# Late x and u tiles transposed by DMA from SBUF to SBUF, and constant matmuls in long planned TensorE gaps

## The chip, the cores and the metric

One core of one Trainium2 chip. The metric is the device time of one execution in microseconds (us). Executions of the same kernel differ by 2 to 3% here: the kernel before gave 174.18 to 178.64 us in its first four runs. Each run lists its granted TensorE clock and is called fast or slow (over 1.5% above the fastest of its kernel is slow).

## The reference, cut to what matters

A linear attention (4 batches, 8 heads, 768 steps, head size 48), whose output `x` goes through a mixing layer:

```python
y[:, :, t] = einsum(rt, state + (u * kt) vt);  state = wt * state + kt vt     # attention, S = 768
theta = x @ w_theta                                                          # needs x transposed
zr, zi = x * cos(theta), x * sin(theta)
u = x + w_tok_r @ zr + w_tok_i @ zi                                          # over the 768 steps
return u + maximum(u @ w_ch, 0)                                              # needs u transposed
```

The kernel works on 24 chunks of 128 steps (batch b, chunk c; number 6b + c). Each gives one x tile of 128x384 and later one u tile of 128x384. Both must be transposed, as three blocks of 128x128, before the product with `w_theta` or `w_ch`.

Of the kernel before, what the change touches and what calls it, by code (L numbers as in the profile page):

```python
# [43 lines left out]
class Planner:  # L44
# [10 lines left out]
    @staticmethod  # L55
    def key(name):

        kind = re.match("[a-zA-Z]+", name).group(0)
        num = name[len(kind):]
        if kind in ("tok", "un", "ut", "uc", "ml", "fin", "st"):  # L60
            b = int(num[0])
        else:
            b = int(num) // 6 if num and kind not in ("wt", "cwt", "wtr", "wev") else 1
        return kind + "@" + "0113"[min(b, 3)]
# [120 lines left out]
def kernel(  # L185
# [60 lines left out]
    sbp = ctx.enter_context(tc.tile_pool(name="sbp", bufs=1))
# [32 lines left out]
    P = Planner(SLOTS, SHIFT, PENALTY, SLACK)  # L279
# [50 lines left out]
    st = [dict() for _ in range(NT)]  # L330
# [24 lines left out]
    def mk_pair(m_, name, src):  # L355
        b, c = chunks[2 * m_]
# [3 lines left out]
        bf = [Buf(pool, [L, H, D], f32, refs=4 if name in "rk" else 2) for _ in range(2)]  # L360
# [6 lines left out]
        def fn():  # L367
# [32 lines left out]
    def attention(n):  # L400
# [189 lines left out]
        def f_xt():  # L590
            t = get(tx)
            for j in range(NJ):
                nc.tensor.transpose(t[:, j, :], x_all[:, b, c, j * L:(j + 1) * L], ident)  # L593
        o_xt = P.op("PE", 0.17, f_xt, [o_x], [tx, xT], [], prio=pr + OFF["xt"], name=f"xt{n}")

        def f_xc():
            nc.scalar.activation(get(xT), get(tx), AF.Copy)  # L597

        def f_xc_v():
            nc.vector.tensor_copy(get(xT), get(tx))  # L600
        s["o_xc"] = P.op("ACT", 0.38, f_xc, [o_xt], [], [tx], prio=pr + OFF["xc"], name=f"xc{n}",
                         alts=[("DVE", 0.26, f_xc_v, PEN)])
        s["o_x"] = o_x


    def attention_pair(m_):
# [181 lines left out]
        for g, hs in enumerate(halves):  # L788
# [10 lines left out]
            if not last:  # L799
# [99 lines left out]
    def mixing(b, ti):  # L899
# [26 lines left out]
        def f_ut():  # L926
            for j in range(NJ):
                nc.tensor.transpose(get(tx)[:, j, :], get(un)[:, j * L:(j + 1) * L], ident)  # L928
        o_ut = P.op("PE", 0.17, f_ut, [o_un], [tx, uT], [], prio=-1.0, name=f"ut{b}{ti}")

        def f_uc():
            nc.scalar.activation(get(uT), get(tx), AF.Copy)  # L932
# [108 lines left out]
```

## The kernel before: the parts that the change touches

Every piece of work is an operation of a planner: engine, planned duration, dependencies, buffers. The planner simulates the engines with these durations and emits the instructions in that order. In the traces here each engine then runs its own list in that order: TensorE stands still in front of a product that isn't ready (up to 2.5 us in the changed kernel) and doesn't pass it.

```python
LAG = {"PE": 0.21, "ACT": 0.16, "DVE": 0.14, "POOL": 0.10, "SP": 1.5, ...}   # after an operation's end
# ---- an x tile: three transposes on TensorE into PSUM, then a copy to SBUF
def f_xt():
    for j in range(NJ):                                   # NJ = 3
        nc.tensor.transpose(t[:, j, :], x_all[:, b, c, j * L:(j + 1) * L], ident)
o_xt = P.op("PE", 0.17, f_xt, [o_x], [tx, xT], [], ...)
s["o_xc"] = P.op("ACT", 0.38, f_xc, [o_xt], [], [tx], ..., alts=[("DVE", 0.26, f_xc_v, PEN)])
...                                                       # a u tile: the same, from un to uT
# ---- constant matmuls, in issue(): only `lead` = 33 at the start, as FUNTIL = 0
if o.start < until:
    n = min(int(gap * part / 0.056), -(-(target - seen) // 128))
    ...                                                   # (cut) a special rule for the first FCOLD us
    for _ in range(n):
        fill()                                            # 128x128 of zeros, result never read
```

All loads (but two of 1.5 KB), and the stores of the output, are issued by SP's queue: the loads for the attention, the weights, and one store for each u tile.

## Time and profile before

| | kernel before |
|---|---|
| median of the runs on record | 176.13 us (174.18 to 178.64, 4 runs; 174.72 over the first three, which the prediction knew) |
| span in the trace | 175.3 us, mean clock 0.941 (a slow run, 177.04 us) |
| TensorE busy | 158.7 us (91%) |
| last issue of a load | 120.2 us |

The busy rows, windows and groups are shown inside the prediction. Two more parts of the page matter for what follows: the chain of work that ended last, by engine, and the DMA issues (issuer, kind, count, size of each, median us from issue to landing).

```profile
PE 63%; DVE 12%; ACT 12%; DMA 8%; issue 1%; SPq 0%; ACTq 0%; DVEq 0%
...
out_dram<-sb_o SPq DMA_DIRECT2D x24, 192.0 KB, 2.0
in_w<-in_w_dram SPq DMA_DIRECT2D x18, 192.0 KB, 5.3
in_r<-in_r_dram SPq DMA_DIRECT2D x18, 192.0 KB, 4.5
```

`SPq` is the queue that issues DMAs.

### The profile page before, as it was taken

What the parts mean: (1) busy time and instruction counts of PE and PEld (TensorE: products, weight loads), DVE (VectorE), ACT (ScalarE), POOL (GpSimd) and SP (SyncE); (2) the same over time, 40 slices, a digit from 0 to 9 for tenths busy, and PEclk for the clock granted to TensorE, in tenths of its full rate; (3) what the DMA queues carried; (4) which work ended last, traced back from release to release, by engine and by line L of the source; (5) the groups of instructions that cost most, each with busy time, mean ns of one, the idle gap of its engine ahead of it and who ended that gap; (6) DMA issues with size and microseconds to landing.
All of it is one profiled execution on the core that took longest, in us unless ns stands there. A gap on an engine that the chain in (4) does not pass through costs nothing.

```text
span 175.3 us, 4898 instructions
## 1 busy us (share of the span) xinstructions
PE 158.7 (91%) x1919; PEld 104.7 (60%) x1919; DVE 130.5 (74%) x278; ACT 117.7 (67%) x255; POOL 114.0 (65%) x134
## 2 busy tenths in 40 slices
PE   7699898999759999999977999999899999999980
PEld 7257565776536566776643667666566666566640
DVE  4507869797996899867899399869989884645461
ACT  2469689799996987966988049799986924810000
POOL 7388689989759578559799987999789310000000
PEclk9858699999996999999996599999999999999999
DMA  5999998899999999999999979989011012112212
GB/s 115 272 301 264 215 222 203 218 264 238 262 222 256 284 160 309 211 208 197 214 206 192 189 129 199 204 174 217 12 45 46 9 38 76 62 45 90 95 45 90
DMA packets 93768, 29.81 MB, mean 170 GB/s; under 512 B 88369, under 2 KB 92210, under 8 KB 93746
## 3 DMA queue, kind: packets, MB, share of 16 engines
q1 hardware_dynamic: 93344, 29.50, 75.9%
q8 instruction: 15, 0.25, 0.6%
q10 hardware_dynamic: 402, 0.00, 0.1%
q14 instruction: 7, 0.06, 0.1%
HBM read 24.78 MB, written 4.72 MB: 168 GB/s over the span
## 4 chain that ended last, share of the span: by engine, by line
PE 63%; DVE 12%; ACT 12%; DMA 8%; issue 1%; SPq 0%; ACTq 0%; DVEq 0%
PE bank L914 24%; DVE sb_z L891 7%; PE bank L941 6%; DMA sb_w<-in_moe_w_tok_i_dram 4%; PE cum L646 3%; PE bank L877 3%; DMA in_k<-in_k_dram 2%; DMA in_w<-in_w_dram 2%; PE bank L928 2%; PE bank L509 2%; PE bank L572 2%; ACT sb_a L439 2%; PE bank L491 2%; PE bank L493 2%; PE cum L430 2%; PE bank L593 1%
## 5 line engine op out<-in xcount | busy, mean ns | idle before, releaser
L914 PE MATMUL bank<-sb_z,wtokT 128*128 128x384 bf16 x288 | 56.3, 337 | 0.4 <-DVE sb_z L891 0.4
L914 PEld LDWEIGHTS <-wtokT 128*128 128x128 bf16 x288 | 27.2, 100 | 17.5 <-issue 3.2
L485 POOL TENSOR_TENSOR sb_bon<-sb_v,sb_rub 128x384 bf16<-128x384 bf16 x18 | 14.9, 829 | 15.0 <-ACT sb_v L465 8.4
L891 DVE TENSOR_TENSOR sb_z<-x_all,sb_sc 128x768 bf16<-128x768 bf16 x24 | 21.6, 911 | 2.4 <-ACT sb_sc L885 2.4
L923 DVE TENSOR_TENSOR sb_un<-bank,x_all 128x384 bf16<-128x384 f32 x24 | 13.3, 555 | 12.2 <-PE bank L914 12.1
L452 POOL TENSOR_TENSOR sb_k<-in_k,sb_a 128x384 bf16<-128x384 f32 x18 | 19.2, 1069 | 4.7 <-DMA in_k<-in_k_dram 4.7
L476 POOL TENSOR_TENSOR sb_ruk<-sb_ru,in_k 128x384 bf16<-128x384 f32 x18 | 19.2, 1067 | 0.6
L458 POOL TENSOR_TENSOR sb_q<-in_r,sb_a 128x384 bf16<-128x384 f32 x18 | 19.0, 1055 | 0.9 <-DMA in_r<-in_r_dram 0.9
L469 POOL TENSOR_TENSOR sb_ru<-in_r,u_bc 128x384 f32<-128x384 f32 x18 | 18.9, 1051 | 0.0
L439 ACT ACTIVATE sb_a<-cum 128x768 f32<-128x768 f32 x18 | 14.6, 810 | 6.0 <-PE cum L434 5.7
L326 ACT ACT_TABLE_LOAD x12 | 15.4, 1283 | 1.5 <-PEq L1025 1.3
L941 PE MATMUL bank<-wch,sb_uT 128*128 128x384 bf16 x72 | 15.7, 326 | 0.6 <-DVE sb_uT L935 0.6
L946 DVE SCALAR_TENSOR_TENSOR sb_o<-bank,sb_un 128x384 f32<-128x384 f32 x24 | 13.3, 553 | 3.9 <-PE bank L941 3.9
L882 ACT ACTIVATE sb_sc<-bank 128x384 bf16<-128x384 f32 x24 | 12.2, 510 | 4.1 <-PE bank L877 4.1
L932 ACT ACTIVATE sb_uT<-bank 128x384 bf16<-128x384 bf16 x16 | 7.8, 489 | 10.3 <-PE bank L928 10.1
L885 ACT ACTIVATE sb_sc<-bank,hpi 128x384 bf16<-128x384 f32 x24 | 14.6, 607 | 0.0
L877 PE MATMUL bank<-wth,sb_xT 128*128 128x384 bf16 x72 | 14.0, 326 | 0.4 <-DVE x_all L841 0.4
L497 DVE COPY sb_qkt<-bank 128x1024 bf16<-128x1024 bf16 x18 | 12.3, 683 | 1.3 <-PE bank L493 1.1
L514 DVE TENSOR_TENSOR sb_p<-bank,mask_exc 128x512 bf16<-128x512 f32 x18 | 12.3, 681 | 0.9 <-PE bank L509 0.8
L521 DVE TENSOR_TENSOR sb_p<-bank,mask_exc 128x512 bf16<-128x512 f32 x18 | 12.2, 679 | 0.0
L587 DVE TENSOR_TENSOR x_all<-bank,sb_bon 128x192 bf16<-128x192 f32 x36 | 10.9, 346 | 1.3 <-PE bank L572 1.3
L597 ACT ACTIVATE sb_xT<-bank 128x384 bf16<-128x384 bf16 x18 | 8.8, 495 | 4.3 <-PE bank L593 4.2
(131 smaller groups left out, 337.1 us busy)
## 6 DMA issues: line engine op xcount, KB each, us to landing
out_dram<-sb_o SPq DMA_DIRECT2D x24, 192.0 KB, 2.0
in_w<-in_w_dram SPq DMA_DIRECT2D x18, 192.0 KB, 5.3
in_r<-in_r_dram SPq DMA_DIRECT2D x18, 192.0 KB, 4.5
in_k<-in_k_dram SPq DMA_DIRECT2D x18, 192.0 KB, 4.5
in_v<-in_v_dram SPq DMA_DIRECT2D x18, 192.0 KB, 4.6
sb_w<-in_moe_w_tok_r_dram SPq DMA_DIRECT2D x6, 384.0 KB, 4.7
sb_w<-in_moe_w_tok_i_dram SPq DMA_DIRECT2D x6, 384.0 KB, 5.1
in_w<-in_w_dram SPq DMA_DIRECT2D x3, 384.0 KB, 5.1
```

The costliest lines, as they stand in the source:

```text
L326: nc.scalar.preload_act_table_set(name)
L439: nc.scalar.activation(get(a), get(cum)[:, :, :DM], AF.Exp)
L452: nc.gpsimd.tensor_tensor(get(kk)[:, :, :D], s["x_k"](), av(1), op=ALU.mult)
L458: nc.gpsimd.tensor_tensor(get(q)[:, :, :D], s["x_r"](), av(0), op=ALU.mult)
L469: nc.gpsimd.tensor_tensor(get(ru), s["x_r"](), u_bc, op=ALU.mult)
L476: nc.gpsimd.tensor_tensor(get(ruk), get(ru), s["x_k"](), op=ALU.mult)
L485: nc.gpsimd.tensor_tensor(get(bon), get(vb), get(rub).to_broadcast([L, H, D]), op=ALU.mult)
L877: nc.tensor.matmul(get(th), lhsT=get(s["xT"])[:, j, :], rhs=wth[:, j, :], start=(j == 0), stop=(j == NJ - 1))
L885: nc.scalar.activation(get(sc)[:, 0, :], get(th), AF.Sin, bias=hpi)
L891: nc.vector.tensor_tensor(get(zb[b])[:, c], xb, get(sc), op=ALU.mult)
L914: nc.tensor.matmul(get(ac), lhsT=wtokT[:, q_, s_, ti, :], rhs=get(zb[b])[:, s_, q_, :], start=(s_ == 0 and q_ == 0), stop=(s_ == NCH - 1 a ...
L941: nc.tensor.matmul(get(ml), lhsT=get(uT)[:, j, :], rhs=wch[:, j, :], start=(j == 0), stop=(j == NJ - 1))
```

## The change

Its intent: take 17 of 48 tiles' transposes off TensorE, the busiest engine, and use the DMA path, which is nearly idle late in the kernel; and keep TensorE's clock up through long gaps. The tuned priorities were searched anew around it.

```diff
-    FCOLD, FPART, FSPAN, FCOL, FUNTIL = 16.0, 0.6, 1.7, 2250, 0.0
+    FCOLD, FPART, FSPAN, FCOL, FUNTIL = 0.0, 0.5, 3.4, 4600, 130.0     # constant matmuls in gaps
+    XBAR = (11, 22)        # u tiles by DMA
+    XBARX = (16, 22)       # x tiles by DMA
+        def f_xx():
+            for j in range(NJ):
+                nc.sync.dma_start(out=get(xT)[:, j, :], in_=x_all[:, b, c, j * L:(j + 1) * L], transpose=True)
+        if XBARX[0] <= n < XBARX[1]:
+            s["o_xc"] = P.op("SP", 0.9, f_xx, [o_x], [xT], [], ...)
+        else: ...          # as before
+        def f_ux():        # the same for u
+        if XBAR[0] <= b * NCH + ti < XBAR[1]:
+            o_uc = P.op("SP", 0.9, f_ux, [o_un], [uT], [], ...)
-    SHIFT, PENALTY, SLACK, WIN = ...          # (cut) the tuned constants of the planner,
+    SHIFT, PENALTY, SLACK, WIN = ...          # new values
-    sb_xT 9, sb_un 3, sb_uT 3                 # buffers
+    sb_xT 7, sb_un 4, sb_uT 4
```

Two planned durations were corrected too (a pair load 1.46 to 1.6 us, a state update 0.45 to 0.76 us).

More of the change, by code (lines that the diff above doesn't have):

```diff
@@ L59, in key @@
         num = name[len(kind):]
-        if kind in ("tok", "un", "ut", "uc", "ml", "fin", "st"):
+        if kind in ("tok", "un", "ut", "ux", "uc", "ml", "fin", "st"):
             b = int(num[0])
@@ L212 @@
     OFF = {'ln': -2.2, 'cum': -2.1, 'exp': -2.05, 'alt': -2.04, 'q': -1.5, 'k': -1.45, 'v': -1.2, 'ru': -1.3, 'ruk': -1.2, 'rub': -1.2, 'bon': -1.1, 'tqk': -0.9, 'qkt': -0.9, 'p': -0.8, 'm0': -0.7, 'pc': -0.7, 'sel': -1.6, 'y': -0.5, 'x': -0.5, 'xt': -0.4, 'xc': -0.4, 'rk': -1.3, 'rkt': -1.2, 'rkc': -1.2, 'beta': -1.15}
-    SHIFT = {'M': -0.23, 'M@0': 3.78, 'M@1': -3.52, 'M@3': 2.56, 'Mp@0': 0.29, 'S': -3.32, 'S@0': 0.3, 'S@1': -2.09, 'S@3': -3.9, 'Sp@0': -0.07, 'alt': -2.71, 'alt@0': -4.19, 'alt@1': -3.75, 'alt@3': -2.44, 'bc@0': -2.12, 'beta@0': 8.49, 'bon': -7.28, 'bon@0': -7.76, 'bon@1': -1.33, 'bon@3': -11.03, 'cos': -4.6, 'cos@0': -7.82, 'cos@1': -5.2, 'cos@3': -5.64, 'cum': 2.98, 'cum@0': -0.21, 'cum@1': 2.19, 'cum@3': 3.61, 'cump@0': -0.23, 'cwch': 2.19, 'cwch@1': 2.56, 'cwt': -0.63, 'cwt@1': -2.08, 'cwth': 0.26, 'cwth@1': -8.48, 'exp': -7.56, 'exp@0': -11.22, 'exp@1': -7.11, 'exp@3': -1.28, 'fin': 10.83, 'fin@0': 12.05, 'fin@1': 12.34, 'fin@3': 8.58, 'k': -2.66, 'k@0': -15.07, 'k@1': -5.34, 'k@3': -4.01, 'ldk': -0.07, 'ldk@0': 0.25, 'ldk@1': 0.06, 'ldk@3': 0.13, 'ldkp@0': -0.61, 'ldr': -0.52, 'ldr@0': -1.79, 'ldr@1': -0.84, 'ldr@3': -1.05, 'ldrp@0': -1.69, 'ldv': 0.27, 'ldv@0': 0.93, 'ldv@1': 1.13, 'ldv@3': 0.9, 'ldvp@0': 0.88, 'ldw': -1.63, 'ldw@0': -1.67, 'ldw@1': -1.98, 'ldw@3': -0.9, 'ldwp@0': -1.18, 'ln': -1.02, 'ln@0': -1.74, 'ln@1': -4.09, 'ln@3': 1.93, 'm': 1.57, 'm@0': 7.07, 'm@1': 11.91, 'm@3': 13.16, 'ml': 3.16, 'ml@0': -7.78, 'ml@1': -6.19, 'ml@3': -6.65, 'p': 4.22, 'p@0': 8.66, 'p@1': 14.26, 'p@3': 6.5, 'pc': 1.07, 'pc@0': 1.12, 'pc@1': -2.22, 'pc@3': -4.15, 'pp@0': 1.14, 'q': -0.33, 'q@0': -3.4, 'q@1': 0.28, 'q@3': 1.27, 'qkt': 1.93, 'qkt@0': -0.14, 'qkt@1': -5.68, 'qkt@3': -3.58, 'qktp@0': 2.71, 'rk@0': 6.13, 'rkc@0': 2.62, 'rkt@0': -1.07, 'ru': -2.75, 'ru@1': -1.4, 'ru@3': 2.61, 'rub': 1.54, 'rub@1': 3.53, 'rub@3': 6.25, 'ruk': -0.11, 'ruk@1': -0.56, 'ruk@3': 0.5, 'sel': 1.06, 'sel@0': 2.59, 'sel@1': -6.63, 'sel@3': -2.52, 'sin': 1.45, 'sin@0': 4.46, 'sin@1': -0.21, 'sin@3': 0.97, 'st': 0.43, 'st@0': -0.77, 'st@1': 3.72, 'st@3': -4.86, 'th': -5.14, 'th@0': -12.99, 'th@1': -9.62, 'th@3': -9.38, 'toE': -2.74, 'toE@0': -6.59, 'toE@1': -1.75, 'toE@3': -1.04, 'toS': -2.78, 'toS@0': 7.44, 'toS@1': 3.52, 'toS@3': 2.77, 'tok': -3.84, 'tok@0': -5.7, 'tok@1': -7.33, 'tok@3': -2.77, 'tqk': -0.37, 'tqk@0': -8.63, 'tqk@1': -1.82, 'tqk@3': -1.42, 'ubc': 3.86, 'ubc@1': 2.43, 'ublk@1': 8.43, 'ubm': 3.03, 'ubm@1': 3.71, 'uc': -4.81, 'uc@0': 3.89, 'uc@1': -2.11, 'uc@3': 5.25, 'un': 2.42, 'un@0': 2.75, 'un@1': -2.25, 'un@3': -1.11, 'ut': -3.32, 'ut@0': -2.56, 'ut@1': -8.44, 'ut@3': -9.24, 'v': 1.33, 'v@0': 5.45, 'v@1': 5.64, 'v@3': 6.18, 'wch': -0.56, 'wch@1': 1.93, 'wev': 2.67, 'wev@1': 6.99, 'wt': 0.86, 'wt@1': 0.73, 'wth': 0.4, 'wth@1': -1.64, 'wtr': 0.92, 'wtr@1': 2.77, 'x': 1.16, 'x@0': -4.58, 'x@1': 1.61, 'x@3': 1.76, 'xc': 1.62, 'xc@0': 2.07, 'xc@1': 3.0, 'xc@3': 1.78, 'xp@0': -0.04, 'xt': 0.48, 'xt@0': 1.96, 'xt@1': 3.17, 'xt@3': 6.63, 'y': -0.38, 'y@0': -2.78, 'y@1': -0.45, 'y@3': 0.21, 'yp@0': 1.15, 'z': -1.82, 'z@0': -4.53, 'z@1': -8.37, 'z@3': -5.1}
@@ L214 @@
-    PENALTY = {'S': 1.09, 'S@0': 1.12, 'S@1': 0.03, 'S@3': -0.59, 'bc@0': -1.6, 'bon@0': 0.89, 'cwch': -1.71, 'cwch@1': -0.3, 'cwt': 1.34, 'cwt@1': 1.64, 'cwth': 1.85, 'cwth@1': 2.85, 'k': 9.17, 'k@0': 6.71, 'k@1': 5.59, 'k@3': 6.89, 'pc': -1.22, 'pc@0': -2.79, 'pc@1': -4.83, 'pc@3': -6.18, 'qkt': 3.99, 'qkt@0': 1.6, 'qkt@1': 0.86, 'qkt@3': 2.34, 'qktp@0': 0.89, 'rk@0': 10.81, 'rkc@0': 2.27, 'ruk': -1.87, 'ruk@1': -3.89, 'ruk@3': -10.16, 'uc': 1.64, 'uc@0': 0.25, 'uc@1': 4.42, 'uc@3': -1.02, 'wev': -0.04, 'wev@1': 0.23, 'xc': -0.05, 'xc@0': 2.57, 'xc@1': 2.52, 'xc@3': 3.03, 'xp@0': 0.65}
+    SHIFT = {'M': -0.23, 'M@0': 3.78, 'M@1': -2.52, 'M@3': 3.01, 'Mp@0': 1.53, 'S': -3.32, 'S@0': 0.3, 'S@1': 0.63, 'S@3': -4.36, 'Sp@0': 1.4, 'alt': -2.71, 'alt@0': -4.47, 'alt@1': -1.63, 'alt@3': -4.6, 'bc@0': -1.23, 'beta@0': 12.08, 'bon': -7.28, 'bon@0': -5.29, 'bon@1': 0.35, 'bon@3': -8.1, 'cos': -4.6, 'cos@0': -9.33, 'cos@1': -3.49, 'cos@3': -3.96, 'cum': 2.98, 'cum@0': -0.21, 'cum@1': 3.75, 'cum@3': 5.42, 'cump@0': -1.49, 'cwch': 2.19, 'cwch@1': -0.96, 'cwt': -0.63, 'cwt@1': -3.12, 'cwth': 0.26, 'cwth@1': -9.29, 'exp': -7.56, 'exp@0': -10.19, 'exp@1': -4.56, 'exp@3': -1.55, 'fin': 10.83, 'fin@0': 10.99, 'fin@1': 9.97, 'fin@3': 7.33, 'k': -2.66, 'k@0': -18.8, 'k@1': -7.79, 'k@3': -6.46, 'ldk': -0.07, 'ldk@0': 0.25, 'ldk@1': 0.06, 'ldk@3': 0.42, 'ldkp@0': -0.45, 'ldr': -0.52, 'ldr@0': -1.79, 'ldr@1': -0.84, 'ldr@3': 0.67, 'ldrp@0': -0.91, 'ldv': 0.27, 'ldv@0': 0.93, 'ldv@1': 0.84, 'ldv@3': -0.27, 'ldvp@0': 0.3, 'ldw': -1.63, 'ldw@0': -1.67, 'ldw@1': -1.84, 'ldw@3': -0.9, 'ldwp@0': -1.25, 'ln': -1.02, 'ln@0': -1.36, 'ln@1': -1.33, 'ln@3': 6.49, 'm': 1.57, 'm@0': -0.46, 'm@1': 6.1, 'm@3': 7.68, 'ml': 3.16, 'ml@0': -6.91, 'ml@1': -8.02, 'ml@3': -8.42, 'p': 4.22, 'p@0': 8.66, 'p@1': 11.81, 'p@3': 4.5, 'pc': 1.07, 'pc@0': 1.12, 'pc@1': 0.19, 'pc@3': -5.32, 'pp@0': 1.11, 'q': -0.33, 'q@0': -4.36, 'q@1': -1.61, 'q@3': -1.63, 'qkt': 1.93, 'qkt@0': -0.16, 'qkt@1': -6.64, 'qkt@3': -4.47, 'qktp@0': 8.5, 'rk@0': 11.67, 'rkc@0': 2.6, 'rkt@0': 1.02, 'ru': -2.75, 'ru@1': 0.09, 'ru@3': 7.17, 'rub': 1.54, 'rub@1': 2.55, 'rub@3': 4.18, 'ruk': -0.11, 'ruk@1': -0.64, 'ruk@3': 0.54, 'sel': 1.06, 'sel@0': 2.59, 'sel@1': -8.51, 'sel@3': -0.48, 'sin': 1.45, 'sin@0': 8.03, 'sin@1': 7.28, 'sin@3': 7.7, 'st': 0.43, 'st@0': -3.12, 'st@1': -2.28, 'st@3': -8.52, 'th': -5.14, 'th@0': -11.38, 'th@1': -7.14, 'th@3': -9.55, 'toE': -2.74, 'toE@0': -3.59, 'toE@1': 4.98, 'toE@3': 1.37, 'toS': -2.78, 'toS@0': 8.07, 'toS@1': 9.18, 'toS@3': 4.18, 'tok': -3.84, 'tok@0': -3.56, 'tok@1': -5.9, 'tok@3': 0.22, 'tqk': -0.37, 'tqk@0': -7.79, 'tqk@1': -1.84, 'tqk@3': 1.63, 'ubc': 3.86, 'ubc@1': 2.17, 'ublk@1': 10.04, 'ubm': 3.03, 'ubm@1': -2.15, 'uc': -4.81, 'uc@0': 1.88, 'uc@1': -0.32, 'uc@3': 4.71, 'un': 2.42, 'un@0': 3.54, 'un@1': 0.59, 'un@3': 0.94, 'ut': -3.32, 'ut@0': 4.0, 'ut@1': -0.49, 'ut@3': -4.37, 'ux@1': 2.07, 'ux@3': 1.0, 'v': 1.33, 'v@0': 12.47, 'v@1': 13.27, 'v@3': 11.66, 'wch': -0.56, 'wch@1': 1.75, 'wev': 2.67, 'wev@1': 12.33, 'wt': 0.86, 'wt@1': 0.73, 'wth': 0.4, 'wth@1': -1.92, 'wtr': 0.92, 'wtr@1': 3.27, 'x': 1.16, 'x@0': -4.58, 'x@1': 1.58, 'x@3': 0.02, 'xc': 1.62, 'xc@0': 1.0, 'xc@1': 2.04, 'xc@3': -0.4, 'xp@0': -2.67, 'xt': 0.48, 'xt@0': 1.66, 'xt@1': 2.11, 'xt@3': 8.81, 'y': -0.38, 'y@0': -2.78, 'y@1': -1.02, 'y@3': -2.05, 'yp@0': 0.2, 'z': -1.82, 'z@0': 0.57, 'z@1': -4.1, 'z@3': -7.66}
@@ new lines @@
+    PENALTY = {'S': 1.09, 'S@0': 1.12, 'S@1': 0.25, 'S@3': -0.21, 'bc@0': -2.77, 'bon@0': 0.35, 'cwch': -1.71, 'cwch@1': -0.6, 'cwt': 1.34, 'cwt@1': 4.81, 'cwth': 1.85, 'cwth@1': 1.65, 'k': 9.17, 'k@0': 8.13, 'k@1': 8.89, 'k@3': 8.64, 'pc': -1.22, 'pc@0': -2.79, 'pc@1': -6.94, 'pc@3': -12.31, 'qkt': 3.99, 'qkt@0': 0.86, 'qkt@1': 3.26, 'qkt@3': 5.89, 'qktp@0': -1.33, 'rk@0': 9.44, 'rkc@0': 1.39, 'ruk': -1.87, 'ruk@1': -1.91, 'ruk@3': -13.18, 'uc': 1.64, 'uc@0': 1.43, 'uc@1': 5.04, 'uc@3': -1.26, 'wev': -0.04, 'wev@1': -0.16, 'xc': -0.05, 'xc@0': 2.47, 'xc@1': 2.67, 'xc@3': 2.65, 'xp@0': 0.98}
@@ L220 @@
     WAHEAD = 1.0
-    SLACK = (4.32, 5.23)
+    SLACK = (0.0, 5.53)
     FLEAD = 33
     FBEGIN = 5.0
-    FCOLD = 16.0
-    FPART = 0.6
-    FSPAN = 1.7
-    FCOL = 2250
-    FUNTIL = 0.0
+    FCOLD = 0.0
+    FPART = 0.5
+    FSPAN = 3.4
+    FCOL = 4600
+    FUNTIL = 130.0
     PKD = 9.0
@@ L236 @@
     PARTS = 2
-    WIN = {'PE': 0.0, 'ACT': 0.0, 'DVE': 0.05, 'POOL': 0.56, 'SP': 0.12}
+    WIN = {'PE': 0.0, 'ACT': 0.02, 'DVE': 0.0, 'POOL': 0.19, 'SP': 0.0}
     GROUPS = [G0, [(0, 6)], [(0, 6)], G3]
@@ L241 @@
              "sb_a": 3, "sb_alt": 5, "sb_v": 5, "sb_ru": 2, "sb_ruk": 2, "sb_rk": 2, "sb_rkT": 2, "beta": 1, "sb_rub": 2,
-             "sb_bon": 4, "sb_qkt": 4, "sb_p": 3, "sb_S": 3, "sb_SD": 3, "sb_xT": 9, "sb_sc": 3,
-             "sb_z": 3, "sb_w": 3, "sb_wn": 4, "sb_un": 3, "sb_uT": 3, "sb_o": 6}
+             "sb_bon": 4, "sb_qkt": 4, "sb_p": 3, "sb_S": 3, "sb_SD": 3, "sb_xT": 7, "sb_sc": 3,
+             "sb_z": 3, "sb_w": 3, "sb_wn": 4, "sb_un": 4, "sb_uT": 4, "sb_o": 6}
     cpool = ctx.enter_context(tc.tile_pool(name="cpool", bufs=1))
@@ L371, in fn @@
                               in_=src[b, :, c * L:(c + 2) * L, :].rearrange("h (p k) d -> p h (k d)", k=2))
-        o = P.op("SP", 1.46, fn, alloc=bf, prio=2 * m_ - (WAHEAD if name == "w" else 0.0), name=f"ld{name}p{2 * m_}")
+        o = P.op("SP", 1.6, fn, alloc=bf, prio=2 * m_ - (WAHEAD if name == "w" else 0.0), name=f"ld{name}p{2 * m_}")
         for k2 in range(2):
@@ L593, in f_xt @@
                 nc.tensor.transpose(t[:, j, :], x_all[:, b, c, j * L:(j + 1) * L], ident)
-        o_xt = P.op("PE", 0.17, f_xt, [o_x], [tx, xT], [], prio=pr + OFF["xt"], name=f"xt{n}")
         def f_xc():
@@ L600, in f_xc_v @@
             nc.vector.tensor_copy(get(xT), get(tx))
-        s["o_xc"] = P.op("ACT", 0.38, f_xc, [o_xt], [], [tx], prio=pr + OFF["xc"], name=f"xc{n}",
-                         alts=[("DVE", 0.26, f_xc_v, PEN)])
+        def f_xx():
+            for j in range(NJ):
+                nc.sync.dma_start(out=get(xT)[:, j, :], in_=x_all[:, b, c, j * L:(j + 1) * L], transpose=True)
+        if XBARX[0] <= n < XBARX[1]:
+            s["o_xc"] = P.op("SP", 0.9, f_xx, [o_x], [xT], [], prio=pr + OFF["xt"], name=f"xx{n}")
+        else:
+            o_xt = P.op("PE", 0.17, f_xt, [o_x], [tx, xT], [], prio=pr + OFF["xt"], name=f"xt{n}")
+            s["o_xc"] = P.op("ACT", 0.38, f_xc, [o_xt], [], [tx], prio=pr + OFF["xc"], name=f"xc{n}",
+                             alts=[("DVE", 0.26, f_xc_v, PEN)])
         s["o_x"] = o_x
@@ L820, in f_S @@
                                                 get(alt[g])[rows].to_broadcast([DP, NP, D]), op=ALU.mult)
-                s["o_S"] = P.op("DVE", 0.45, f_S, [o_mm, s["o_alt"]], [], [m, alt[g]], prio=pr - 0.6, name=f"Sp{n}")
+                s["o_S"] = P.op("DVE", 0.76, f_S, [o_mm, s["o_alt"]], [], [m, alt[g]], prio=pr - 0.6, name=f"Sp{n}")
             def f_y(g=g, c=c, hs=hs, ys=ys, prev=prev):
@@ L928, in f_ut @@
                 nc.tensor.transpose(get(tx)[:, j, :], get(un)[:, j * L:(j + 1) * L], ident)
-        o_ut = P.op("PE", 0.17, f_ut, [o_un], [tx, uT], [], prio=-1.0, name=f"ut{b}{ti}")
         def f_uc():
@@ L935, in f_uc_v @@
             nc.vector.tensor_copy(get(uT), get(tx))
-        o_uc = P.op("ACT", 0.38, f_uc, [o_ut], [], [tx], prio=-1.0, name=f"uc{b}{ti}",
-                    alts=[("DVE", 0.26, f_uc_v, PEN)])
+        def f_ux():
+            for j in range(NJ):
+                nc.sync.dma_start(out=get(uT)[:, j, :], in_=get(un)[:, j * L:(j + 1) * L], transpose=True)
+        if XBAR[0] <= b * NCH + ti < XBAR[1]:
+            o_uc = P.op("SP", 0.9, f_ux, [o_un], [uT], [], prio=-1.0, name=f"ux{b}{ti}")
+        else:
+            o_ut = P.op("PE", 0.17, f_ut, [o_un], [tx, uT], [], prio=-1.0, name=f"ut{b}{ti}")
+            o_uc = P.op("ACT", 0.38, f_uc, [o_ut], [], [tx], prio=-1.0, name=f"uc{b}{ti}",
+                        alts=[("DVE", 0.26, f_uc_v, PEN)])
         def f_ml():
```

## The prediction

> **What bounds the kernel now.** I first read the page's slices (part 2), in which each digit is a tenth of one of 40 slices of 4.4 us.
>
> ```profile
> PE   7699898999759999999977999999899999999980
> DVE  4507869797996899867899399869989884645461
> POOL 7388689989759578559799987999789310000000
> PEclk9858699999996999999996599999999999999999
> DMA  5999998899999999999999979989011012112212
> ```
>
> TensorE is full nearly everywhere. POOL and the loads stop at about 139 and 123 us, while TensorE goes on to the end, so the last quarter is pure TensorE work. The clock row has four dips to half speed. I then cut the span at these places with a table of windows; its columns are the window, its length, busy time and instructions by engine, granted clock, DMA share and GB/s.
>
> ```profile
> 8.00:15.00 7.00, 7.00 (x47) 4.00 (x46) 1.50 (x2) 4.33 (x9) 6.05 (x7) 0.52 1.22 286
> 18.00:22.00 4.00, 3.95 (x45) 2.60 (x46) 3.21 (x5) 2.32 (x11) 2.46 (x3) 0.57 0.96 205
> 42.00:52.50 10.50, 7.14 (x92) 5.15 (x92) 10.50 (x18) 10.47 (x21) 7.43 (x8) 0.99 0.93 217
> 52.50:56.00 3.50, 3.50 (x29) 2.30 (x28) 2.77 (x6) 2.70 (x4) 3.39 (x5) 0.55 1.09 260
> 89.00:93.50 4.50, 2.26 (x30) 1.21 (x28) 4.50 (x8) 3.75 (x8) 4.42 (x4) 0.96 0.87 184
> 93.50:100.00 6.50, 6.22 (x33) 3.52 (x34) 3.97 (x9) 2.31 (x5) 6.50 (x8) 0.50 1.29 198
> 100.00:123.00 23.00, 22.95 (x301) 15.48 (x300) 20.28 (x41) 18.48 (x46) 20.58 (x22) 1.00 0.97 184
> 123.00:129.00 6.00, 4.91 (x71) 3.31 (x70) 6.00 (x12) 5.50 (x15) 4.38 (x5) 1.00 0.02 4
> 129.00:171.30 42.30, 41.68 (x375) 26.22 (x373) 27.58 (x57) 17.05 (x37) 9.02 (x10) 1.00 0.16 58
> ```
>
> From 129 to 171.3 us TensorE is busy 41.68 of 42.3 us: a TensorE instruction taken out there should shorten the end by its own length. From 100 to 123 us it is as full, but DVE, ACT and POOL are above 80% too and the DMA queue is at 0.97. Each clock dip follows a stretch with a loose TensorE (3.4 us idle in 42 to 52.5, 2.2 us in 89 to 93.5). The lost array time is (1 - clock) x length: 3.4 us in 8-15, 1.7 in 18-22, 1.6 in 52.5-56, 3.2 in 93.5-100, together some 9.9 us. Last I read the order of time in the tail and the cost groups of the operations that the change touches.
>
> ```profile
> 154.87 0.33 PE L928 MATMUL bank<-ident,sb_un 128*128 128x128 bf16 x3
> 155.03 1.14 PE L914 MATMUL bank<-sb_z,wtokT 128*128 128x384 bf16 x6
> 156.01 0.65 PE L941 MATMUL bank<-wch,sb_uT 128*128 128x384 bf16 x3
> ```
>
> ```profile
> L928 PE MATMUL bank<-ident,sb_un 128*128 128x128 bf16 x72 | 8.0, 219 | 0.9 <-DVE sb_un L923 0.9
> L932 ACT ACTIVATE sb_uT<-bank 128x384 bf16<-128x384 bf16 x16 | 7.8, 489 | 10.3 <-PE bank L928 10.1
> L597 ACT ACTIVATE sb_xT<-bank 128x384 bf16<-128x384 bf16 x18 | 8.8, 495 | 4.3 <-PE bank L593 4.2
> ```
>
> The three transposes of a tile start at 154.87 and the next product at 155.03: a tile's transposes take 0.16 to 0.17 us of the TensorE stream. The 8.0 us busy of that group overstates them, because matmuls overlap. Taking the tile out of PSUM afterwards costs 0.49 us on ACT (or 0.36 on DVE).
>
> **What the Trainium skill says.** "TensorE: Matmul & The Clock Gate", Part 1, says that an idle window of about 3.4 us returns the array to half clock, and that 128-column matmuls then follow each other at 107 ns instead of 56. The trace agrees in kind: granted clock 0.50 after the loose stretch at 89-93.5. "VectorE: DVE Perf Modes", "The three transpose paths", gives 390 ns for a 128x128 bf16 transpose on TensorE into PSUM and 1309 ns by the DMA's crossbar, straight into SBUF. In this stream TensorE's costs 0.055 us each; no run here shows the DMA's. "Advanced Engine Details and Errata", "X-Bar Transpose (TRN2)", says that transposing DMAs are as fast as ordinary ones and that only one stream of them may be in flight; all here go out on SP's queue. The only ordinary DMAs of the trace with an idle queue are the stores of the tail, 2.0 us from issue to landing; loads take 4.5 to 5.3 us, because they queue.
>
> **The change, part by part.** (1) Chunks 16 to 21 of x and u tiles 11 to 21 (17 of 48 tiles) lose three TensorE transposes each, 51 in all, and their copies. Instead SP issues three 32 KB transposing DMAs for each tile. 17 x 0.165 = 2.8 us of TensorE stream. In the kernel before, u tiles 11 to 21 all stand after 129 us (13 of the 24 groups do), as do 5 of the x groups, of which 3 are moved: (11 + 3) x 0.165 = 2.3 us in the saturated tail. The other three x tiles lie before 129 us, where TensorE is full, but others share the limit; I count half, 0.25 us. The last two u tiles stay on TensorE, so the final chain after 169.7 us (transpose, copy, product, 0.56 us on DVE, store) keeps its length.
>
> (2) The copies: 17 x 0.49 = 8.3 us of mostly ACT time, late. By the instruction order, ACT's copies of uT fall from 16 to 11 and of xT from 24 to 18, DVE's of uT from 8 to 2; ACT gets four more of state scaling and 16 more of the bonus products (two tiles), DVE three more weight copies. So DVE is relieved only a little. Its full 6.0 us in 123-129, with 1.1 us of TensorE idle, may ease: 0.4 us.
>
> (3) Constant matmuls: both kernels start with 33. The order shows 62 more, not about 45, in 12 places, all within the first 1340 of 3860 TensorE instructions, the first third of the stream. They aim at the dips at 8-15, 18-22 and 52.5-56, not at the one of 93.5-100. Fully cured, the second and third are worth 3.3 us of array time; since up to 56 us ACT, DVE and the loads are close to full too, I take 35%: 1.2 us. Cost: 62 x 0.056 to 0.107 = 3.5 to 6.6 us, nearly all in planned idle time; 0.3 us for those that come late.
>
> (4) The whole order was tuned anew for the new durations. The bubble at 89-100 (2.2 us idle, 3.2 us cold) hangs on that order and on DVE's z products; after the change the order has the same mix of theta products and attention there. I take 0.7 us of its 5.4 as gained, an unsupported guess of the sign.
>
> (5) New costs: before the last loads the SP order has four x tiles, 12 DMAs. 96 KB at the 184 KB/us of that stretch is 0.5 us of the queue for each, 2.1 us in all, if small pieces go no slower. Loads then come later, and the POOL work behind them; the tail has 42 us of TensorE work, so perhaps 0.6 us shows. The latency of a tile rises from 0.17 + 0.49 us plus hand-overs to some 2.5 to 3.5 us (an estimate: 2.0 us of a store, plus three issues of 0.4 us or more, the shortest load issue in the trace). Products wait in order; the plan sets 1 to 4 groups of L914 (0.98 us each) between, so mostly hidden: 0.4 us of stalls.
>
> Sum: -2.3 - 0.25 - 0.4 - 1.2 + 0.3 - 0.7 + 0.6 + 0.4 = -3.55 us, from 174.72 to 171.2. As the order was retuned around the new operations, I lean a little lower and set 170.9.
>
> **The rivals.** (A) The DMA transposes become the new wait: if a tile takes 4 us or more instead of 2.5 to 3.5, TensorE stalls at many of the 11 products of the tail, in order, and SP's queue holds back stores and loads behind it. Against it: the queue is at 0.16 after 129 us. For it: nothing in this trace shows such a DMA, and 1309 ns each, if not overlapped, would be 3.9 us a tile. Half a microsecond at each of 11 products costs 5 us: 175 to 178. (B) The clock is the real prize: if the constant matmuls remove two dips and the new order closes the bubble at 89-100, then 3.3 + 5.4 us are at stake and the time is 165 to 168. Against it: no filler stands near that bubble. (C) Only the tail's transposes count and the fillers do nothing, because the early part is bound by loads (DMA share about 1.0 up to 123 us): 172 to 173, within 2%.
>
> **Range and chances.** The middle of my sum lies on the 2% line (171.2). Runs of the kernel before spread from 174.18 to 178.64, and the profiled one is called slow (177.04), so I allow for noise in the medians. Range 166.8 to 175.0. Faster by over 2%: 0.57; within 2%: 0.35; slower: 0.08, almost all of it rival A.
>
> **What would show it.** Step 1: from the last POOL work to the end TensorE stays full with a clock of 1.00, and has 51 transposes less. Step 3: the clock row keeps its nines at 18-22 and 52-56; if the dips stay, 1.2 us of the sum is wrong. Step 5: the issue-to-landing time of the transposing DMAs, and TensorE's idle time before the L955 products by releaser DMA; over 2 us in all is rival A. Loads ending much later than 123 us show the queue cost. I am wrong if the new order moves the bubble, if a transposing DMA takes far longer than a store, or if SP's issue time for one is over a microsecond.

## The result, and the profile after

The changed kernel takes 212.66 us (median, 211.32 to 214.64, 4 runs) against 176.13 us. The ratio is 1.2165, with a 95% interval of 1.1956 to 1.2373. A ratio here is the mean of one kernel's fast runs over the mean of the other's fast runs of the same rounds, so not quite the ratio of the medians. The change costs some 36 us; the prediction had it 4 us faster.

The slices of the changed kernel (5.2 us each):

```profile
PE   7796986959697999999999996867862997793592
POOL 7487288929640999994599994664710000000000
PEclk9979799979969999999999999699667599997588
DMA  6999998875999899999999335734121222111142
```

TensorE, full to the end before, has holes from the 25th slice on, and the clock falls again and again there. The DMA engines aren't the limit: their share is 1 to 4 tenths in the last third. The chain and the product that reads the transposed u show where the time went (columns of a group: busy us, mean ns of one, idle time before it and what ended it):

```profile
PE 35%; SPq 19%; ACT 16%; POOL 11%; DMA 8%; DVE 5%; issue 4%; POOLq 0%; ACTq 0%; DVEq 0%
SPq L945 14%; PE bank L922 10%; DMA sb_uT<-sb_un 5%; SPq L604 3%; POOL sb_q L460 3%; POOL sb_k L454 3%; PE cum L1023 3%; PE bank L955 3%; PE cum L654 2%; ACT sb_sc L893 2%; PE bank L1004 2%; ACT sb_a L441 2%; PE bank L885 2%; POOL sb_ru L471 2%; DMA in_w<-in_w_dram 2%
...
L955 PE MATMUL bank<-wch,sb_uT 128*128 128x384 bf16 x72 | 20.9, 358 | 18.0 <-DMA sb_uT<-sb_un 17.6
```

SP's queue is now 19% of the chain, where it was 0%. L945 and L604 are the lines that issue the transposing DMAs. TensorE stands idle 17.6 us directly in front of the u product, waiting for them. The views of the two tiles give the duration of each issue (ns, min/median/max) and its landing; the last line holds for the u tile:

```profile
L604 SPq DMA_TRANSPOSE sb_xT<-x_all x18: 1096/1226/2599, 114.6 to 155.8; - x18
L945 SPq DMA_TRANSPOSE sb_uT<-sb_un x33: 1093/1226/1589, 140.5 to 198.7; - x33
...
DMA to landing us min/median/max: 2.2/2.3/3.1
```

This is the key reading. A transposing DMA lands 2.3 us after its issue begins, much as a store does (2.1 us here). But SP is held 1.226 us for each one, where the stores of this trace hold it 0.52 us. A tile is three of them, which SP issues one after the other: 3.7 us of SP for a tile, and 51 x 1.226 = 62.5 us for all. SP's order of time shows it (start, length, how many):

```profile
114.64 3.72 SPq L604 DMA_TRANSPOSE sb_xT<-x_all  x3
118.41 0.58 SPq L351 DMA_DIRECT2D in_v<-in_v_dram  x1
119.09 0.53 SPq L351 DMA_DIRECT2D in_w<-in_w_dram  x1
119.71 5.11 SPq L604 DMA_TRANSPOSE sb_xT<-x_all  x3
124.92 0.52 SPq L964 DMA_DIRECT2D out_dram<-sb_o  x1
125.55 0.38 SPq L351 DMA_DIRECT2D in_k<-in_k_dram  x1
...
184.48 15.48 SPq L945 DMA_TRANSPOSE sb_uT<-sb_un  x12
```

Two harms follow. First, from 114.6 us on, loads stand behind transposes in SP's list: the last load is issued at 144.4 us instead of 120.2, and POOL waits longer for `in_r`, in the kernel before and in the changed one (total us, times, longest):

```profile
POOL sb_q L458 <- DMA in_r<-in_r_dram: 0.9, 1, 0.9
POOL sb_q L460 <- DMA in_r<-in_r_dram: 10.0, 4, 3.9
```

Second, in the tail TensorE is paced by SP, block by block:

```profile
189.68 0.34 PE L955 MATMUL bank<-wch,sb_uT 128*128 128x384 bf16 x1 [0.97 <-DMA sb_uT<-sb_un]
190.92 0.50 PE L955 MATMUL bank<-wch,sb_uT 128*128 128x384 bf16 x1 [0.91 <-DMA sb_uT<-sb_un]
192.22 0.50 PE L955 MATMUL bank<-wch,sb_uT 128*128 128x384 bf16 x1 [0.80 <-DMA sb_uT<-sb_un]
193.53 0.50 PE L955 MATMUL bank<-wch,sb_uT 128*128 128x384 bf16 x1 [0.81 <-DMA sb_uT<-sb_un]
```

One third of a product every 1.24 to 1.31 us: SP's pace, 12 issues in 15.48 us or 1.29 us for each. In the kernel before, a whole tile of the tail (twelve L914 matmuls, transposes, product) took some 2.6 us (160.24 to 162.85 us in its trace); SP alone now needs 3.7. The clock falls too, which stretches what is left: it is 1.00 from 114 to 129 us, where TensorE is full, and 0.70 to 0.90 in the stretches from there to 206 us, where it is 64 to 85% busy. In the kernel before it was 1.00 from 129 to 171 us.

### The profile page after: what moved, and what is told of

It is laid out like the page before. It is cut to its first block, busy times and chain, and to the rows that moved or that the text cites. A ratio compares the mean times of both kernels' runs of the same rounds, so it can differ in the third digit from the quotient of the medians.

```text
span 209.6 us, 5011 instructions
## 1 busy us (share of the span) xinstructions
PE 170.2 (81%) x1930; PEld 107.6 (51%) x1930; DVE 124.0 (59%) x272; ACT 117.9 (56%) x263; POOL 110.4 (53%) x132
## 4 chain that ended last, share of the span: by engine, by line
PE 35%; SPq 19%; ACT 16%; POOL 11%; DMA 8%; DVE 5%; issue 4%; POOLq 0%; ACTq 0%; DVEq 0%
SPq L945 14%; PE bank L922 10%; DMA sb_uT<-sb_un 5%; SPq L604 3%; POOL sb_q L460 3%; POOL sb_k L454 3%; PE cum L1023 3%; PE bank L955 3%; PE cum L654 2%; ACT sb_sc L893 2%; PE bank L1004 2%; ACT sb_a L441 2%; PE bank L885 2%; POOL sb_ru L471 2%; DMA in_w<-in_w_dram 2%
## 5 line engine op out<-in xcount | busy, mean ns | idle before, releaser
L922 PE MATMUL bank<-sb_z,wtokT 128*128 128x384 bf16 x288 | 57.8, 348 | 1.4 <-ACT sb_xT L861 1.2
L922 PEld LDWEIGHTS <-wtokT 128*128 128x128 bf16 x288 | 28.1, 104 | 20.7 <-issue 6.7
L955 PE MATMUL bank<-wch,sb_uT 128*128 128x384 bf16 x72 | 20.9, 358 | 18.0 <-DMA sb_uT<-sb_un 17.6
L460 POOL TENSOR_TENSOR sb_q<-in_r,sb_a 128x384 bf16<-128x384 f32 x18 | 19.1, 1062 | 20.3 <-ACT sb_alt L446 10.3
L955 PEld LDWEIGHTS <-sb_uT 128*128 128x128 bf16 x72 | 6.5, 99 | 28.2 <-DMA sb_uT<-sb_un 25.5
L899 DVE TENSOR_TENSOR sb_z<-x_all,sb_sc 128x768 bf16<-128x768 bf16 x24 | 16.4, 698 | 7.4 <-ACT sb_sc L893 7.2
L1023 PE MATMUL cum<-warm 128*128 128x128 bf16 x95 | 10.8, 286 | 6.9 <-ACT sb_a L441 2.0
L885 PE MATMUL bank<-wth,sb_xT 128*128 128x384 bf16 x72 | 16.0, 363 | 0.4 <-ACT sb_sc L893 0.4
L597 ACT ACTIVATE sb_xT<-bank 128x384 bf16<-128x384 bf16 x12 | 6.0, 500 | 16.0 <-PE bank L595 16.0
L516 DVE TENSOR_TENSOR sb_p<-bank,mask_exc 128x512 bf16<-128x512 f32 x18 | 12.3, 685 | 2.7 <-PE bank L511 2.7
L1023 PEld LDWEIGHTS <-warm 128*128 128x128 bf16 x95 | 9.2, 132 | 7.0 <-issue 5.5
```

The lines of the kernel that those rows point to most:

```text
L460: nc.gpsimd.tensor_tensor(get(q)[:, :, :D], s["x_r"](), av(0), op=ALU.mult)
L885: nc.tensor.matmul(get(th), lhsT=get(s["xT"])[:, j, :], rhs=wth[:, j, :], start=(j == 0), stop=(j == NJ - 1))
L899: nc.vector.tensor_tensor(get(zb[b])[:, c], xb, get(sc), op=ALU.mult)
L922: nc.tensor.matmul(get(ac), lhsT=wtokT[:, q_, s_, ti, :], rhs=get(zb[b])[:, s_, q_, :], start=(s_ == 0 and q_ == 0), stop=(s_ == NCH - 1 a ...
L955: nc.tensor.matmul(get(ml), lhsT=get(uT)[:, j, :], rhs=wch[:, j, :], start=(j == 0), stop=(j == NJ - 1))
L1023: nc.tensor.matmul(wps, lhsT=warm[:, 0, :], rhs=warm[:, 1, :], start=True, stop=True)
```

## The experiments

All twelve kernels were correct. Theory S: the cost is the issuer's time for each transposing instruction. Rivals: the new order and the constant matmuls did it (T), or the crossbar and DMA path itself are slow (D).

| run | kernel | median us (range, runs) | ratio to before (95%) |
|---|---|---|---|
| e1 | changed, no transposing DMA | 180.7 (176.07 to 180.98, 4) | unresolved |
| e2 | old tuning, 51 DMAs | 203.43 (201.97 to 204.76, 4) | 1.157 (1.143 to 1.170) |
| e3 | changed, one DMA for a tile | 177.95 (177.35 to 180.83, 4) | 1.011 (1.001 to 1.021) |
| e4 | changed, DMAs issued by ACT | 211.04 (209.56 to 213.72, 4) | 1.194 (1.178 to 1.210) |
| e5 | old tuning, one DMA for a tile | 174.54 (173.03 to 177.29, 6) | 0.993 (0.986 to 1.000) |
| e6 | e3 without constant matmuls in gaps | 177.45 (176.03 to 181.46, 6) | 1.009 (1.001 to 1.017) |
| e7 | before + constant matmuls in gaps | 176.85 (176.38 to 177.97, 6) | 1.010 (1.004 to 1.016) |
| e8 | changed, only the x tiles by DMA (18) | 184.79 (184.13 to 185.36, 4) | 1.055 (1.048 to 1.062) |
| e9 | changed, only the u tiles by DMA (33) | 198.17 (197.47 to 198.87, 2) | 1.128 (1.121 to 1.136) |
| e10 | e5, only the u tiles by DMA | 175.51 (173.93 to 176.26, 6) | 0.999 (0.994 to 1.004) |
| e11 | e5, planner told 1.2 us for a tile | 173.15 (172.13 to 175.88, 6) | 0.984 (0.980 to 0.988) |
| e12 | e10, planner told 1.2 us for a tile | 173.97 (172.76 to 175.99, 6) | 0.987 (0.982 to 0.992) |

The kernel before had medians of 176.88 us (e1 to e4), 175.6 us (e5 to e8) and 175.35 us (e9 to e12) in these rounds. An edit that changes what is planned lets the planner re-order; e3 and e4 keep the changed kernel's plan, e6 keeps e3's, and e7 that of the kernel before.

### e1: no transposing DMA

```diff
-    XBAR = (11, 22);  XBARX = (16, 22)
+    XBAR = (99, 99);  XBARX = (99, 99)
```

> All 17 tiles go back to TensorE and a copy; new tuning, new slots and constant matmuls stay. Theory S (SP spends 1.23 us on each of 51 transposing DMAs, 63 us of its queue, and that is the whole loss): the time falls back to 172 to 180 us. Rival T (the new order and the constant matmuls lost the time: the changed kernel was behind on the scan well before its first transposing DMA): it stays above 190 us.

Measured 180.7 us; three runs at 180.5 to 181.0, all called slow, and one at 176.07, so no clean ratio. The transposing DMAs bring 32 to 37 us of the loss. T as the main cause is refuted; that the rest of the change costs a few us is not.

### e2: the old tuning with the 51 DMAs

```diff
-    SHIFT, PENALTY, SLACK, WIN, F... = new values
+    SHIFT, PENALTY, SLACK, WIN, F... = those of the kernel before    # the two planned durations too
```

> The same 17 tiles by DMA, but all tuning constants and the absence of constant matmuls as in the kernel before (only the buffer counts are the new ones). Theory S: 203 to 217 us, as the 63 us of SP are the same. Rival T: 175 to 185 us.

203.43 us, at the lower end of what S expected. The loss comes with the DMAs, whatever the tuning, though the old order loses 9 us less.

### e3: one DMA for a tile

```diff
-            for j in range(NJ):
-                nc.sync.dma_start(out=get(uT)[:, j, :], in_=get(un)[:, j * L:(j + 1) * L], transpose=True)
+            nc.sync.dma_start(out=get(uT), in_=get(un), transpose=True)          # 128x384; x the same
```

> The changed kernel with one transposing DMA of 128x384 for each tile instead of three of 128x128; the planned order is the same. If SP's 1.23 us is a cost of an instruction, SP needs some 1.3 us for a tile and the kernel falls to 175 to 188 us. If it is a cost of each 128x128 block, SP needs some 3.5 us for a tile and the time stays at 207 to 214 us.

177.95 us. The same bytes, tiles, engines and planned order, 17 instructions instead of 51, and 34.7 us of median time are gone. The tile views of this run (u, then x):

```profile
L943 SPq DMA_TRANSPOSE sb_uT<-sb_un x11: 1181/1194/2026, 129.2 to 163.7; - x11
...
DMA to landing us min/median/max: 2.3/2.3/3.2
...
L603 SPq DMA_TRANSPOSE sb_xT<-x_all x6: 1187/1258/1702, 113.6 to 139.1; - x6
```

A transpose of 128x384 holds SP 1.19 us and lands after 2.3 us, as one of 128x128 did (these are the u tiles; the x tiles, issued beside the loads, hold it 1.26 us and land after 3.1 us). So the cost belongs to the instruction, not to the block, and rival D falls: the crossbar takes three blocks in the time of one. The last load goes out at 130.6 us instead of 144.4.

### e4: the DMAs on ACT's queue

```diff
-                nc.sync.dma_start(out=get(uT)[:, j, :], ..., transpose=True)
+                nc.scalar.dma_start(out=get(uT)[:, j, :], ..., transpose=True)   # x the same
```

> The changed kernel with its 51 transposing DMAs issued by ACT instead of SP. Theory S (the issuer is blocked, the crossbar itself is quick): SP's loads are no longer held back, ACT pays the 63 us instead, of which some lies in its idle time: 185 to 205 us, loads done by about 130 us instead of 146. Rival D (the crossbar or the DMA queue itself is slow, whoever issues): 207 to 214 us, as the tiles land no earlier.

211.04 us: my expectation for S missed, and D's number was met, for another reason. The trace shows the same cost on the other queue, and ACT's own work behind it (columns as above; ACTq is ACT's queue):

```profile
149.37 3.89 ACTq L604 DMA_TRANSPOSE sb_xT<-x_all  x3
153.35 3.78 ACTq L945 DMA_TRANSPOSE sb_uT<-sb_un  x3
157.24 0.49 ACT L890 ACTIVATE sb_sc<-bank 128x384 bf16<-128x384 f32 x1 [6.68 <-DMA sb_uT<-sb_un]
```

The median issue was 1.252 us. The loads did get earlier (last `in_k` issued at 132.8 us instead of 140.0), but ACT's sine stood up to 6.7 us behind transposes, and DVE then waited 19.1 us in all for ACT's cosines (7.2 us in the changed kernel). Who issues isn't the point; that each instruction holds its issuer is. I had counted ACT's idle time and not the chain that runs through ACT.

### e8 and e9: x tiles alone, u tiles alone (three DMAs each)

```diff
e8:  XBAR = (99, 99)
e9:  XBARX = (99, 99)
```

> The changed kernel with only the six x tiles by DMA, three instructions each (18 DMAs, 22 us of SP, all beside the last loads); the u tiles are back on TensorE. If the loads held behind the transposes are the larger part of the loss: 190 to 205 us. If the tail's products that wait for 33 transposes are the larger part: 180 to 188 us.

> The changed kernel with only the eleven u tiles by DMA, three instructions each (33 DMAs, 41 us of SP, nearly all after the loads). Theory S: the tail is then paced by SP, a tile every 3.7 us for eleven tiles, so 190 to 205 us; TensorE waits in front of the u products for more than 12 us. If the x tiles and the held loads were most of the loss: 180 to 187 us.

e8 took 184.79 us, e9 198.17 us. Against the 177.95 us of e3, x costs some 7 to 8 us and u some 20 us (the rounds differ, and e3 still has 17 DMAs, so these are sizes and not exact parts); so the paced tail is the larger harm, as e9's text said; of e8's two ranges, the one met is the one for the tail too. They sum to less than the 35 us of all 51; the likely reason, that delayed loads push the attention and with it the tail's tiles later, no run shows. In e8 the POOL engine waits 8.8 us for `in_r`; in e9, with the loads out by 126.1 us, TensorE waits for transposing DMAs (I expected over 12 us):

```profile
PE bank L955 <- DMA sb_uT<-sb_un: 13.4, 18, 1.1
```

### e5, e6, e7: what tuning and constant matmuls bring

```diff
e5:  e2 with one DMA for a tile
e6:  e3 with  FUNTIL = 0.0
e7:  the kernel before with  FCOLD, FPART, FSPAN, FCOL, FUNTIL of the changed kernel   (54 more constant matmuls)
```

> The same as the old-tuning run (17 tiles by DMA, no constant matmuls in gaps), with one transposing DMA for a tile instead of three. Theory I (1.2 us of the issuer for each instruction; nothing else is wrong with the DMA path): 17 x 1.2 = 20 us of SP fit beside its other work, the TensorE tail loses its 2.3 to 2.8 us, and the time is 172 to 175 us where the kernel before of the same rounds has about 176.5. Rival L (a tile's latency of 2.3 us and more still stalls the products in order): 177 to 182 us.

> The changed kernel with one DMA for a tile and without the 62 constant matmuls in gaps; the planned order is the same as with them. The prediction's step: they save about 0.9 us net, so 178.5 to 180 us. Rival F (they come late, at half clock and in front of real work, and cost more than they bring): 174 to 177 us.

> The kernel before with the rule for constant matmuls alone (54 more, four of them near the dip at 93 us); its planned order is unchanged. The prediction's step: 1 to 3 us faster than the kernel before. Rival F: the same or up to 3 us slower.

e5 beats its e2 by 29 us (S again), and stands at 0.993. e3 stands at 1.011, so what else is new in e3 (order, planned durations, constant matmuls) costs about 1.8%; that it does because the order was made for durations that the chip doesn't have is argued, not shown. e6 against e3: 1.009 and 1.011, no difference that intervals of about 1% each can show; 177.45 us lies between the two ranges I had written. e7 is 1.0% slower than the kernel before. The window that holds the old dip, in the kernel before and in e7 (length, TensorE busy, clock, DMA share, GB/s):

```profile
89.00:100.00 11.00, 8.48 (x63) 0.69 1.12 192
```

```profile
89.00:100.00 11.00, 8.80 (x121) 1.00 1.22 192
```

It looks as if the constant matmuls had cured the dip. The other traces don't bear that out. Only 4 of the 54 stand near this dip (at 94.95 us in e7). And e5, which has none in gaps, runs TensorE's instructions from 86 to 101 us in the same order as the kernel before, with the same idle gaps in front of them (0.71, 1.08 and 0.72 us), and at full clock:

```profile
93.50:100.00 6.50, 6.50 (x78) 4.24 (x79) 6.46 (x14) 4.04 (x9) 6.50 (x8) 1.00 1.39 195
```

The line of the kernel before for this window is in the prediction: 33 matmuls, clock 0.50. Of the other kernels with the old tuning and no constant matmuls in gaps, e2 and e11 have 1.00 there, e10 0.74 and e12 0.53; the kernel before and e12 were profiled in slow runs, the others in fast ones. So the dip comes and goes between traces without any constant matmuls, and e7 doesn't show that they cured it.

Nor is a dip there without cost. From POOL's 17th `sb_k` to its 20th (94.00 to 111.99 us in the kernel before) it took 17.99 us in the kernel before and 17.94 in e12, 16.73 in e10, and 15.73 or 15.74 in e2, e5, e7 and e11. e7 gains 2.25 us in this stretch, but came to it 1.97 us late; from 53 to 58 us its clock was 0.50 to 0.57, where the kernel before was back at 1.00 after 56 us. From the 20th `sb_k` on the two traces are alike: POOL starts its last `sb_k` at 134.3 and 133.9 us, and TensorE is busy 41.38 and 41.30 us from 129 to 171 us. What a cured dip is worth is therefore not measured, and where e7's 1% comes from, I did not settle.

### e10, e11, e12: a version that beats both

```diff
e10:  e5 with XBARX = (99, 99)
e11:  e5 with  P.op("SP", 0.9, f_xx / f_ux)  ->  P.op("SP", 1.2, ...)
e12:  both
```

> Old tuning, one DMA for a tile, only the eleven u tiles (no transposing DMA beside the loads but one or two). If the x tiles in the load phase cost what their 6 x 0.165 us bring: 172 to 174.5 us and faster than the old tuning with both. If not: 174 to 176 us.

> Old tuning, one DMA for a tile, both x and u, with the planner told 1.2 us of SP for a tile (measured) instead of 0.9. If the 2.6 us of TensorE waits for transposing DMAs in the tail come from the plan's too short figure: the waits fall under 1.5 us and the time to 172 to 173.5 us. If they come from SP's order (transposes behind stores): no change, 174 to 175.5 us.

> Both of the last two edits: only the u tiles, one DMA each, 1.2 us in the plan. 171.5 to 174 us if either helps; not below 171, since all that can be gained is 11 x 0.165 = 1.8 us of the tail and a dip of the clock.

e10 (0.999) missed its range: as far as these intervals tell, six x tiles by DMA cost nothing net, so removing them gains nothing. e11 is the best kernel, 0.984 of the kernel before (0.980 to 0.988), 2.8 us of 175.35. e12 is 0.987, and the two aren't told apart. The waits of TensorE's queues for the u transposes, in e5 and then in e11 (total, times, longest us):

```profile
PEld L953 <- DMA sb_uT<-sb_un: 4.3, 5, 1.7
PE bank L953 <- DMA sb_uT<-sb_un: 2.6, 3, 1.4
```

```profile
PEld L953 <- DMA sb_uT<-sb_un: 2.2, 4, 0.9
PE bank L953 <- DMA sb_uT<-sb_un: 0.7, 2, 0.5
```

With 1.2 us in place of 0.9, the plan leaves more room before each product and TensorE's wait falls from 2.6 to 0.7 us, as expected of that theory (under 1.5). That this is what e11 gains isn't shown: the two profiled runs took 173.03 (e5) and 173.14 us (e11), and the intervals of e5 and e11 overlap.

## Why the prediction was wrong

**The step that failed is part (5), "New costs".** It took "three issues of 0.4 us or more, the shortest load issue in the trace". A transposing issue takes 1.226 us. From this come both errors of that part. The latency of a tile, put at 2.5 to 3.5 us, comes to 2 x 1.226 + 2.3 = 4.8 us, an estimate from these measured parts. Worse, the part never summed SP's time: it counted latency, and bytes of the DMA queue, but not that 51 x 1.226 = 62.5 us have to pass through one in-order queue in some 85 us (114.6 to 200.0), together with the loads. "0.6 us shows" for delayed loads became some 7 to 8 us (e8 against e3), and "0.4 us of stalls" about 20 us (e9 against e3).

**Rival A had the right mechanism and the wrong size.** It named the products that wait in order and the queue that holds back loads, and put it at 175 to 178 us; the chance was 0.08. It too counted a delay for each product (0.5 us) and not a rate: SP needs 3.7 us for a tile, TensorE some 2.6. Its argument against, a DMA share of 0.16 after 129 us, looked at the DMA engines; the busy resource was the queue in front of them, which the busy rows don't show.

**Parts (1) and (2), the gain.** Parts (1) and (2) came to -2.95 us. With the instruction count mended, e11 gains 2.8 us. The size agrees, but e11 also differs from the kernel before in its plan and in its clock dips, so this isn't a measurement of the removed transposes alone.

**Part (3), constant matmuls: -0.9 us net.** The first step that failed is "fully cured". The prediction's own sign was a clock row that keeps its nines at 18-22 and 52-56. In the changed kernel the clock is 0.78 from 18 to 22 us; the dip at 52.5-56 is gone, but 56 to 60 us has 0.73. The second is the reading of the dips: they were taken from one trace, of a slow run, as the kernel's own, and the one at 93.5-100, which the prediction ties to the loose stretch before it, is not there in e5 after the same stretch. At the end no gain shows: e6 and e3 don't differ, e7 is 1% slower. Whether 35% of the lost array time reaches the end stays open; at 93.5-100 a dip put at 3.2 us goes with 2.25 us of POOL's chain. Rival C, in which the constant matmuls do nothing, had the result; its reason, the loads, isn't shown.

**Part (4), the retuned order.** "An unsupported guess of the sign" was a wrong one: e3 against e5 puts the new tuning, constant matmuls included, at about 1.8% slower (e6 against e5, without them, at 1.6%). "As the order was retuned around the new operations, I lean a little lower" took the search for a measurement. What it was tuned to is a plan in which a tile costs SP 0.9 us and is there 1.5 us later. That sum, 2.4 us, is right for one DMA of a whole tile (2.3 us), and wrong by half for the three that the code issues.

Of the signs that the prediction named, the last was the one that mattered: "if SP's issue time for one is over a microsecond".

## What to carry to other kernels

Before moving work to DMAs, multiply the number of DMA instructions by what one holds its issuer, and compare it with the time that the issuer's queue has: low use of the DMA engines says nothing about the queue in front of them. Where the cost is for an instruction, make fewer and larger ones; here a single edit of the loop brought back 35 us. And before you plan the cure of a clock dip, look at more than one trace, of fast runs: the same TensorE instructions with the same gaps ran at 0.50 in one trace and at 1.00 in another.

## What the Trainium skill lacked or had wrong

- "DMA: Bandwidth & Descriptors", "DMA Transpose (X-bar)": it has no figure for what one transposing DMA from SBUF to SBUF holds its issuer on trn2 (a table elsewhere on the page, set against trn3, has only a count for 8,192 tiles on "previous generations"). Measured: 1.226 us on SP, 1.252 us on ACT for 128x128 bf16, and 1.19 us on SP for 128x384 (u tiles), so by the instruction. Whether the issuer works in this time or waits for hardware behind it, the runs don't tell.
- The same page, "Issuing engines are not separate DMA queues", says that the time on the sequencer to initiate a DMA is "usually small relative to the DMA itself". For these DMAs it was 1.2 of 2.3 us, and it set the pace of the kernel.
- "Advanced Engine Details and Errata", "X-Bar Transpose (TRN2)": "TRN2 transpose DMAs are as fast as regular DMAs". By landing this holds (2.3 us for 32 KB, 2.1 us for a store of 192 KB in the same trace); by issue it does not (1.226 us, a store 0.52 us).
- "VectorE: DVE Perf Modes", "The three transpose paths", gives 1309 ns for 128x128 by the DMA crossbar. Measured from issue to landing: 2.3 us for 128x128, and 2.3 us for 128x384 (u tiles). From where to where the page's figure runs, it doesn't say.
- "TensorE: Matmul & The Clock Gate", Part 1, gives an idle window of about 3.4 us for the return to half clock. Here 2.2 to 2.5 us of idle time within 4.5 us were followed by a clock of 0.50 in one trace (the kernel before) and of 1.00 in another (e5). The page calls its window free-running, which would allow both; no run here shows that this is the reason. That constant matmuls keep the clock up, e7 does not show.
